# Attention scores by three one-pass matmuls of split q and k, with four float64 conversions moved behind the first two experts

## The chip, the cores and the metric

One core of a Trainium2 chip runs the whole program. The metric is the device time of one execution in microseconds; lower is better. TensorE is called PE here (its weight loads PEld), VectorE DVE, ScalarE ACT, GpSimd POOL, SyncE SP.

## The reference

Three layers run one after the other on 1792 tokens of 768 numbers. First an attention of 4 batches and 12 heads with a sigmoid in place of softmax, then a mixture of 8 experts to which tokens are given greedily by logit, 224 to each, then a dense layer with a squared relu:

```python
scores = scale * np.matmul(q, k.transpose(0, 1, 3, 2)) - np.log(S)   # q, k, v: (4, 12, 448, 64)
attn = 1.0 / (1.0 + np.exp(-scores))
x = np.matmul(attn, v)                      # then reshaped to (1792, 768)
...
h = np.maximum(x[mask] @ w1[e], 0.0)        # expert e, w1 (768, 1024), w2 (1024, 768)
out[mask] = h @ w2[e]
...
r = np.maximum(x @ w_in, 0.0)               # w_in (768, 2048), w_out (2048, 768)
out = (s * (r * r) + b) @ w_out
```

The weights of the dense layer, `w_in` and `w_out`, come as float64 bits; the kernel makes float32 of them itself, in 32 units of 128x768 numbers.

## The kernel before, in words

The program is written in one order (a manual schedule), and each engine runs its own instructions in that order. **Attention** is a loop over 24 head pairs i (6 pairs of each batch). A pair's q and k lie transposed with head 0 on partitions 0 to 63 and head 1 on 64 to 127, so a score matmul contracts over 64 rows, one half of the array for each head. In `scores` (L225) a chunk is 112 keys by 448 queries of both heads: two float32 matmuls on the two row halves (L235) into one PSUM tile `psc`, of which there are three, then one sigmoid on ACT (L236). A pair has four chunks. In `values` (L240) eight float32 matmuls make `pv` from the four chunks, and ACT copies it to `xT` (L253). Iteration i issues: the load of q and k of pair i+4, of v of pair i+3, `values(i)`, then the last two chunks of pair i+1 and the first two of pair i+2. The four chunks between two `values` are called a phase below.

In the same loop DVE makes float32 of the float64 units, `convert` (L155): four DVE instructions each (`to_float`, L148), a load of 768 KB ahead (`craw`) and a store of 384 KB behind (`nw`). The list CONV (L44) says how many in each iteration: 26 in all. The last LATE = 6 units are converted later (`late_convert`, L718), in one buffer called `orow`: its load is issued right behind the store of the conversion before.

After attention come the choice of experts, the gather of rows (`gather`, L531), and then four groups g. **A group** computes two experts, then the dense layer for their 448 tokens: 16 hidden blocks f (L743 to L761), each of 18 one-pass matmuls of 448 columns (L706 to L708), and two halves h of 8 spans (L768 to L797), each of 18 matmuls of 384 columns in group 0. All weights stream through SBUF in units: SP loads `raw` (L181), ACT rounds it to `wh` (L189, type float32r, one pass on PE), and `w_low` makes the rest `wl` = raw - wh (L200), on DVE for all units of the dense layer. `advance` (L666), called at the end of each block and span, keeps `wl` four units ahead of PE's use. Of a hidden block DVE also squares (L750) and makes the low part of `gt` (L755), which waits for ACT's high part (L754). In group 0 late conversions stand behind `advance` of blocks f = 1, 4, 7, 10, 13 and of the first span of half 0:

```python
advance()
if not g and f % 3 == 1:
    late_convert()
```

Unit 16 is that of the first span, unit 19 that of the fourth; block f's `advance` makes DVE split unit f + 4.

Of the kernel before, what the change touches and what calls it, by code (L numbers as in the profile page):

```python
# [8 lines left out]
F32 = mybir.dt.float32  # L9
F32R = mybir.dt.float32r  # L10
BF16 = mybir.dt.bfloat16
I32 = mybir.dt.int32
# [7 lines left out]
B, H, S, D = 4, 12, 448, 64  # L20
# [4 lines left out]
CP = 112  # L25
# [15 lines left out]
ROWS = (2, 2, 2, 2, 2, 2, 2, 2, 2, 2)  # L41
SYNC = 4
SIGNS = 2
CONV = [1, 1, 1, 1, 2] * 4 + [1, 1, 0]  # L44
LATE = 6
FULL = CAP - 0.5
BIG = 1.0e30
FLATC = 16384.0
# [14 lines left out]
def tile_kernel(ctx, tc, qT, kT, v, wg, w1, w2, wi, wo, s2, b2, cst, out):  # L63
    nc = tc.nc
    V, A, G, T = nc.vector, nc.scalar, nc.gpsimd, nc.tensor
# [51 lines left out]
    cgp = early.enter_context(tc.tile_pool(name="cgp", bufs=1))  # L117

    att = ExitStack()
    qk = att.enter_context(tc.tile_pool(name="qk", bufs=5))  # L120
    vp = att.enter_context(tc.tile_pool(name="vp", bufs=2))
    at = att.enter_context(tc.tile_pool(name="at", bufs=2))
    ps_s = att.enter_context(tc.tile_pool(name="ps_s", bufs=3, space=PSUM))
# [11 lines left out]
    def cv_in():  # L135
        if todo:
            i = todo.pop(0)
            src, k, n = wide[i]
            craw[i] = cgp.tile([128, 768, 2], I32, name="craw", bufs=3)
            nc.sync.dma_start(craw[i].rearrange("p a b -> p (a b)"), src[n].bitcast(I32).rearrange("p k c -> p (k c)"))  # L140
            coming.append(i)
# [64 lines left out]
        nu["use"] += 1  # L206
        return splits.pop(i)

    raw_qk, vt, attn, plg, lgs, pts = {}, {}, {}, {}, {}, {}
    pairs = [(b, p) for b in range(B) for p in range(NP)]  # L210

    def load_v(i):
        b, p = pairs[i]
        vt[i] = vp.tile([CP, NC, 128], F32, name="vt", bufs=5)
        nc.sync.dma_start(vt[i], v[b, p])

    def load_qk(i):
        b, p = pairs[i]
        rk = qk.tile([128, S], F32, name="rk")
        nc.sync.dma_start(rk, kT[b, p])  # L220
        rq = qk.tile([128, S], F32, name="rq")
        nc.sync.dma_start(rq, qT[b, p])
        raw_qk[i] = (rq, rk)

    def scores(n, c0, c1):  # L225
        if n >= len(pairs):
            return
        if c0 == 0:
            attn[n] = at.tile([CP, 2, NC, S], F32, name="attn")
        rq, rk = raw_qk[n]  # L230
        for c in range(c0, c1):
            p = ps_s.tile([CP, 2, 512], F32, name="psc")
            for j in range(2):
                me = slice(j * D, (j + 1) * D)
                T.matmul(p[:, j, :S], rk[me, c * CP:(c + 1) * CP], rq[me], start=True, stop=True)  # L235
            A.activation(attn[n][:, :, c, :], p[:, :, :S], AF.Sigmoid, bias=nls[:CP], scale=1.0 / math.sqrt(D))  # L236
        if c1 == NC:
            raw_qk.pop(n)

    def values(i):  # L240
        a, v = attn.pop(i), vt.pop(i)
# [95 lines left out]
    load_v(2)  # L337
    cv_in()
    cv_in()
    scores(0, 0, NC)  # L340
    scores(1, 0, 2)
    nc.sync.dma_start(sb2[:, 0:1], s2.partition_broadcast(128))
# [13 lines left out]
    for i in range(N):  # L356
        b, p = pairs[i]
        if i + 4 < N:
            load_qk(i + 4)
        if i + 3 < N:  # L360
            load_v(i + 3)
        values(i)
        scores(i + 1, 2, NC)
        scores(i + 2, 0, 2)
        if p == 0 and b:
            gate_turn(b - 1, True)
            prefs(b - 1)
        elif p == 4:
            gate(b, 0, 4 if b < B - 1 else 5, 6 if b < B - 1 else 5)
            if b == B - 1:  # L370
                gate_copy(b)
        elif p == 5 and b < B - 1:
            gate(b, 4, 6, 6)
            gate_copy(b)
        if b == B - 1 and 1 <= p <= 3:
            bracket(p - 1)
        if N - 6 <= i < N - 2:
            w_dma()
        if i >= N - 4:
            w_high()  # L380
            w_low(G)
        if i < N - 1:
            for _ in range(CONV[i]):
                convert()
# [343 lines left out]
        x_split(0, n)  # L728
    gather(1)
    row_ids()  # L730
    for g in range(4):
        y = ml.tile([128, KD, 2, S], F32R, name="y")
        expert(2 * g, y)
# [3 lines left out]
        if not t0:  # L737
            gt = ml.tile([128, KG, 2, 512], F32R, name="gt")
        gn = gt[:, :, :, t0:t0 + S]
        if not g:  # L740
            last["buf"] = ml.tile([128, 3072], I32, name="orow")
            late_in()
        for f in range(KG):  # L743
            wh, wl = w_get()
            p = ps_m.tile([128, 512], F32, name="acc")
            for k in range(KD):
                full_mm(p[:, :S], wh[:, k], wl[:, k], y, k, k == 0, k == KD - 1)
            r = m2p.tile([128, S], F32, name="r")
            A.activation(r, p[:, :S], AF.Relu)  # L749
            V.scalar_tensor_tensor(r, r, sb2[:, 0:1], r, op0=ALU.mult, op1=ALU.mult)  # L750
            if g:
                V.tensor_scalar(gn[:, f, 0], r, sb2[:, 1:2], None, op0=ALU.add)
            else:
                A.activation(gn[:, f, 0], r, AF.Identity, bias=sb2[:, 1:2])  # L754
            V.scalar_tensor_tensor(gn[:, f, 1], r, sb2[:, 1:2], gn[:, f, 0].bitcast(F32),  # L755
                                   op0=ALU.add, op1=ALU.subtract)
            if f % 4 == 3:
                x_split(2 * g + 2, f // 4)
            advance()
            if not g and f % 3 == 1:  # L760
                late_convert()  # L761
        gather(2 * g + 3)
        tiles = [(128 * t, idt[:, t - 1, g:g + 1]) for t in range(1, 4)]
# [4 lines left out]
        for h in range(2):  # L768
# [3 lines left out]
            for span in spans:  # L772
# [20 lines left out]
                        elif h:  # L793
                            out_rows.append((ids, orow[:, t]))
                advance()
                if not g and not h and span == [0]:
                    late_convert()  # L797


# [62 lines left out]
```

## Time and profile before

| what | value |
|---|---|
| time, median of 3 runs | 955.37 us (954.41 to 956.3) |
| the profiled execution's own time | 954.64 us |
| its span in the profile | 952.9 us |
| mean granted clock of PE | 0.976 |
| PE busy, share of the span | 926.7 us, 97% |
| weight loads (PEld) | 784.7 us, 82% |
| DVE | 554.8 us, 58% |
| ACT | 450.9 us, 47% |
| POOL | 137.7 us, 14% |

PE is busy nearly throughout, so the time is what PE has to run plus the stretches in which it waits. The shares of the other engines are means over stages: attention takes the first 170 us, the choice of experts some 45, the four groups the rest. Matmul records overlap (the next one starts before the last has left the array), so what one costs is read from the distance of starts, not from its duration.

### The profile page before, as it was taken

How to read it: one execution, taken by the hardware profiler on the slowest of the kernel's cores; microseconds unless marked ns; L12 is line 12 of the kernel's file. 1: busy time of each engine (PE TensorE's matmuls, PEld its weight loads, DVE VectorE, ACT ScalarE, POOL GpSimd, SP SyncE). 2: the span in 40 equal slices, each digit the busy share in tenths (PEclk: the TensorE clock that was granted, in tenths of full speed). 3: DMA queues.
4: the chain of work that ended last, by engine and by line, in shares of the span. 5: the costliest groups of instructions: out<-in, count | busy, mean ns of one | idle time of the engine just before them, and what ended most of it. 6: DMA issues, size and time to landing. Idle time of an engine off the chain costs nothing.

```text
span 952.9 us, 14071 instructions
## 1 busy us (share of the span) xinstructions
PE 926.7 (97%) x5277; PEld 784.7 (82%) x5277; DVE 554.8 (58%) x999; ACT 450.9 (47%) x787; POOL 137.7 (14%) x136
## 2 busy tenths in 40 slices
PE   9999999778999999999999999999999999999997
PEld 3333433557899999999999999999999999999997
DVE  3453736653876885387677223776773287777320
ACT  6665657644664443466433124664333366533120
POOL 1000001324410000433000003420000242100001
PEclk9999999758999999999999999999999999999999
DMA  9979776553675665477433324774444376443411
GB/s 294 376 251 367 277 278 237 151 157 134 206 225 183 218 213 192 143 240 230 146 116 117 125 87 138 244 230 131 119 127 145 119 240 207 136 132 103 128 36 66
DMA packets 68456, 173.08 MB, mean 182 GB/s; under 512 B 7968, under 2 KB 24864, under 8 KB 68384
## 3 DMA queue, kind: packets, MB, share of 16 engines
q1 hardware_dynamic: 64256, 160.22, 51.9%
q0 software_dynamic: 2272, 11.01, 3.4%
q10 hardware_dynamic: 1856, 0.92, 0.3%
q8 instruction: 42, 0.69, 0.3%
q14 instruction: 30, 0.25, 0.1%
HBM read 148.52 MB, written 23.59 MB: 181 GB/s over the span
## 4 chain that ended last, share of the span: by engine, by line
PE 84%; DVE 5%; DMA 5%; issue 2%; ACT 2%; POOL 1%; POOLq 0%; ACTq 0%; SPq 0%; DVEq 0%
PE acc L640 9%; PE acc L706 8%; PE acc L707 8%; PE acc L708 8%; PE psc L235 8%; PE acc L780 8%; PE acc L782 8%; PE acc L781 8%; PE pv L245 8%; PE acc L641 4%; DMA raw<-in_w_dram 4%; DVE wl L200 3%; PE px L407 2%; ACT wh L189 1%; DMA xr<-xs,idx 1%
## 5 line engine op out<-in xcount | busy, mean ns | idle before, releaser
L189 ACT CAST wh<-raw 128x768 fp32r<-128x768 f32 (+1 forms) x240 | 209.0, 878 | 155.8 <-PE acc L782 125.8
L200 DVE TENSOR_TENSOR wl<-raw,wh 128x768 fp32r<-128x768 f32 (+1 forms) x198 | 209.5, 1064 | 97.2 <-ACT wh L189 97.2
L200 POOL TENSOR_TENSOR wl<-raw,wh 128x768 fp32r<-128x768 f32 (+1 forms) x42 | 91.6, 2188 | 422.7 <-ACT wh L189 422.6
L780 PE MATMUL acc<-wh,gt 128*128 128x384 f32 x448 | 149.9, 335 | 0.0
L782 PE MATMUL acc<-wh,gt 128*128 128x384 f32 x448 | 149.7, 334 | 0.0
L781 PE MATMUL acc<-wl,gt 128*128 128x384 f32 x448 | 149.7, 334 | 0.0
L706 PE MATMUL acc<-y,wh 128*128 128x448 f32 x384 | 141.2, 368 | 0.0
L708 PE MATMUL acc<-y,wl 128*128 128x448 f32 x384 | 140.4, 366 | 0.0
L707 PE MATMUL acc<-y,wh 128*128 128x448 f32 x384 | 140.4, 366 | 0.0
L640 PE MATMUL acc<-u,wh 128*128 128x448 f32 x384 | 122.1, 376 | 3.5 <-DVE u L664 3.2
L641 PE MATMUL acc<-u,wl 128*128 128x224 f32 x384 | 101.5, 264 | 0.0
L236 ACT ACTIVATE attn<-psc,nls 112x896 f32<-112x896 f32 x96 | 89.0, 1009 | 13.7 <-PE psc L235 13.7
L640 PE MATMUL acc<-x,wh 128*128 128x448 f32 x288 | 95.2, 385 | 0.0
L749 ACT ACTIVATE r<-acc 128x448 f32<-128x448 f32 x64 | 34.8, 544 | 116.1 <-PE acc L708 116.1
L781 PEld LDWEIGHTS acc<-wl,gt 128*128 128x128 f32 x448 | 84.1, 188 | 0.0
L780 PEld LDWEIGHTS acc<-wh,gt 128*128 128x128 f32 x448 | 84.1, 188 | 0.0
L782 PEld LDWEIGHTS acc<-wh,gt 128*128 128x128 f32 x448 | 84.1, 188 | 0.0
L640 PEld LDWEIGHTS acc<-u,wh 128*128 128x128 f32 x384 | 72.0, 188 | 10.9 <-DVE u L664 5.7
L235 PE MATMUL psc<-rq,rk 64*112 64x448 f32 x384 | 78.8, 549 | 0.0
L641 PE MATMUL acc<-x,wl 128*128 128x224 f32 x288 | 77.2, 268 | 0.9 <-POOL wl L200 0.9
L245 PE MATMUL pv<-attn,vt 112*64 112x448 f32 x384 | 77.5, 545 | 0.0
L708 PEld LDWEIGHTS acc<-y,wl 128*128 128x128 f32 x384 | 72.1, 188 | 5.9
(207 smaller groups left out, 1223.2 us busy)
## 6 DMA issues: line engine op xcount, KB each, us to landing
raw<-nw SPq DMA_DIRECT2D x128, 384.0 KB, 3.1
raw<-in_w_dram SPq DMA_DIRECT2D x64, 384.0 KB, 3.2
raw<-in_w_dram SPq DMA_DIRECT2D x48, 512.0 KB, 4.4
craw<-in_wi_dram SPq DMA_DIRECT2D x16, 768.0 KB, 8.6
nw<-co SPq DMA_DIRECT2D x26, 384.0 KB, 7.5
craw<-in_wo_dram SPq DMA_DIRECT2D x10, 768.0 KB, 8.6
rk<-in_kT_dram SPq DMA_DIRECT2D x24, 224.0 KB, 8.4
rq<-in_qT_dram SPq DMA_DIRECT2D x24, 224.0 KB, 8.4
```

Of the source, the lines that this page charges most:

```text
L189: A.copy(h[:, :k], raws[i][:, :k])
L200: eng.tensor_sub(lo[:, :k], r[:, :k], h[:, :k].bitcast(F32))
L235: T.matmul(p[:, j, :S], rk[me, c * CP:(c + 1) * CP], rq[me], start=True, stop=True)
L245: T.matmul(pv[j * 64:(j + 1) * 64, :S], v[:, c, j * D:(j + 1) * D], a[:, j, c, :], start=(c == 0), stop=(c == NC - 1))
L640: T.matmul(p[:, :2 * CAP], wh[:, k], src[:, k].rearrange("p a s -> p (a s)"), start=(k == 0), stop=False)
L641: T.matmul(p[:, :CAP], wl[:, k], src[:, k, 0], start=False, stop=(k == n - 1))
L706: T.matmul(p, wh, src[:, k, 0], start=first, stop=False)
L707: T.matmul(p, wh, src[:, k, 1], start=False, stop=False)
L708: T.matmul(p, wl, src[:, k, 0], start=False, stop=last)
L780: T.matmul(ps[t][:, :DH], hi, wh[:, cols], start=(f == 0), stop=False)
L781: T.matmul(ps[t][:, :DH], hi, wl[:, cols], start=False, stop=False)
L782: T.matmul(ps[t][:, :DH], lo, wh[:, cols], start=False, stop=(f == KG - 1))
```

## The change

Of pairs 2 to 23, DVE splits q and k when they are loaded (`split_qk`): a high part in float32r and the low rest, both heads and both of q and k in one 128x896 instruction each, kept in the rings of the weight splits `wh` and `wl` (five tiles each). A chunk's two float32 matmuls become six in float32r: high by high, low k by high q, high k by low q, each on both row halves. Pairs 0 and 1 stay as they were. The split of pair i+3 stands at the start of iteration i, ahead of that iteration's conversion; q and k of a pair share one tile, four of them in the ring. CONV becomes one conversion in each of 22 iterations, LATE becomes 10: four more units are converted in group 0, behind blocks f = 0, 2, ..., 14 and behind spans 0 and 2 of the first half. The first late load is issued ahead of expert 0 and no longer behind expert 1.

```diff
@@ -41,8 +41,9 @@
 ROWS = (2, 2, 2, 2, 2, 2, 2, 2, 2, 2)
 SYNC = 4
 SIGNS = 2
-CONV = [1, 1, 1, 1, 2] * 4 + [1, 1, 0]
-LATE = 6
+CONV = [1] * 22 + [0]
+LATE = 10
+PLAIN = 2
 FULL = CAP - 0.5
 BIG = 1.0e30
 FLATC = 16384.0
@@ -117,7 +118,7 @@
     cgp = early.enter_context(tc.tile_pool(name="cgp", bufs=1))
 
     att = ExitStack()
-    qk = att.enter_context(tc.tile_pool(name="qk", bufs=5))
+    qk = att.enter_context(tc.tile_pool(name="qk", bufs=4))
     vp = att.enter_context(tc.tile_pool(name="vp", bufs=2))
     at = att.enter_context(tc.tile_pool(name="at", bufs=2))
     ps_s = att.enter_context(tc.tile_pool(name="ps_s", bufs=3, space=PSUM))
@@ -206,7 +207,7 @@
         nu["use"] += 1
         return splits.pop(i)
 
-    raw_qk, vt, attn, plg, lgs, pts = {}, {}, {}, {}, {}, {}
+    raw_qk, two_qk, vt, attn, plg, lgs, pts = {}, {}, {}, {}, {}, {}, {}
     pairs = [(b, p) for b in range(B) for p in range(NP)]
 
     def load_v(i):
@@ -216,26 +217,40 @@
 
     def load_qk(i):
         b, p = pairs[i]
-        rk = qk.tile([128, S], F32, name="rk")
-        nc.sync.dma_start(rk, kT[b, p])
-        rq = qk.tile([128, S], F32, name="rq")
-        nc.sync.dma_start(rq, qT[b, p])
-        raw_qk[i] = (rq, rk)
+        r = qk.tile([128, 2, S], F32, name="rqk")
+        nc.sync.dma_start(r[:, 1], kT[b, p])
+        nc.sync.dma_start(r[:, 0], qT[b, p])
+        raw_qk[i] = r
+
+    def split_qk(i):
+        r = raw_qk.pop(i)
+        h = wsp.tile([128, 8, 128], F32R, name="wh").rearrange("p k c -> p (k c)")[:, :2 * S]
+        lo = wlp.tile([128, 8, 128], F32R, name="wl").rearrange("p k c -> p (k c)")[:, :2 * S]
+        r = r.rearrange("p a s -> p (a s)")
+        V.tensor_copy(h, r)
+        V.tensor_sub(lo, r, h.bitcast(F32))
+        two_qk[i] = [a.rearrange("p (a s) -> p a s", a=2) for a in (h, lo)]
 
     def scores(n, c0, c1):
         if n >= len(pairs):
             return
         if c0 == 0:
             attn[n] = at.tile([CP, 2, NC, S], F32, name="attn")
-        rq, rk = raw_qk[n]
+        if n < PLAIN:
+            terms = [(raw_qk[n], raw_qk[n])]
+        else:
+            h, lo = two_qk[n]
+            terms = [(h, h), (lo, h), (h, lo)]
         for c in range(c0, c1):
             p = ps_s.tile([CP, 2, 512], F32, name="psc")
-            for j in range(2):
-                me = slice(j * D, (j + 1) * D)
-                T.matmul(p[:, j, :S], rk[me, c * CP:(c + 1) * CP], rq[me], start=True, stop=True)
+            for m, (kx, qx) in enumerate(terms):
+                for j in range(2):
+                    me = slice(j * D, (j + 1) * D)
+                    T.matmul(p[:, j, :S], kx[me, 1, c * CP:(c + 1) * CP], qx[me, 0], start=(m == 0),
+                             stop=(m == len(terms) - 1))
             A.activation(attn[n][:, :, c, :], p[:, :, :S], AF.Sigmoid, bias=nls[:CP], scale=1.0 / math.sqrt(D))
         if c1 == NC:
-            raw_qk.pop(n)
+            (raw_qk if n < PLAIN else two_qk).pop(n)
 
     def values(i):
         a, v = attn.pop(i), vt.pop(i)
@@ -337,6 +352,7 @@
     load_v(2)
     cv_in()
     cv_in()
+    split_qk(2)
     scores(0, 0, NC)
     scores(1, 0, 2)
     nc.sync.dma_start(sb2[:, 0:1], s2.partition_broadcast(128))
@@ -359,6 +375,8 @@
             load_qk(i + 4)
         if i + 3 < N:
             load_v(i + 3)
+        if i + 3 < N:
+            split_qk(i + 3)
         values(i)
         scores(i + 1, 2, NC)
         scores(i + 2, 0, 2)
@@ -728,6 +746,8 @@
         x_split(0, n)
     gather(1)
     row_ids()
+    last["buf"] = ml.tile([128, 3072], I32, name="orow")
+    late_in()
     for g in range(4):
         y = ml.tile([128, KD, 2, S], F32R, name="y")
         expert(2 * g, y)
@@ -737,9 +757,6 @@
         if not t0:
             gt = ml.tile([128, KG, 2, 512], F32R, name="gt")
         gn = gt[:, :, :, t0:t0 + S]
-        if not g:
-            last["buf"] = ml.tile([128, 3072], I32, name="orow")
-            late_in()
         for f in range(KG):
             wh, wl = w_get()
             p = ps_m.tile([128, 512], F32, name="acc")
@@ -757,7 +774,7 @@
             if f % 4 == 3:
                 x_split(2 * g + 2, f // 4)
             advance()
-            if not g and f % 3 == 1:
+            if not g and f % 2 == 0:
                 late_convert()
         gather(2 * g + 3)
         tiles = [(128 * t, idt[:, t - 1, g:g + 1]) for t in range(1, 4)]
@@ -793,7 +810,7 @@
                         elif h:
                             out_rows.append((ids, orow[:, t]))
                 advance()
-                if not g and not h and span == [0]:
+                if not g and not h and span in ([0], [2]):
                     late_convert()
```

How it moves instructions, at three places. First PE, one phase of attention ahead of a `values` (names: `psc` a score chunk, `rq`/`rk` q and k, `wh`/`wl` their high and low parts, `pv` the values). Before, two matmuls make a chunk:

```order
L245 MATMUL pv_345<-attn_280,vt_210 64x448 x8
L235 MATMUL psc_355<-rq_208,rk_206 112x448 x2
L235 MATMUL psc_359<-rq_208,rk_206 112x448 x2
L235 MATMUL psc_364<-rq_258,rk_256 112x448 x2
L235 MATMUL psc_368<-rq_258,rk_256 112x448 x2
```

and now six, in three steps of two row halves; here the first three of a phase's four chunks:

```order
L260 MATMUL pv_500<-attn_404,vt_311 64x448 x8
L249 MATMUL psc_510<-wh_374 112x448 x2
L249 MATMUL psc_510<-wh_374,wl_375 112x448 x2
L249 MATMUL psc_510<-wl_375,wh_374 112x448 x2
L249 MATMUL psc_518<-wh_374 112x448 x2
L249 MATMUL psc_518<-wh_374,wl_375 112x448 x2
L249 MATMUL psc_518<-wl_375,wh_374 112x448 x2
L249 MATMUL psc_527<-wh_435 112x448 x2
L249 MATMUL psc_527<-wh_435,wl_436 112x448 x2
L249 MATMUL psc_527<-wl_436,wh_435 112x448 x2
```

Nothing changes places on PE; each chunk has three pairs of matmuls for one.

Second DVE, iteration 12 of attention (`L` to `Wp` are the gate preferences of a batch, which wait for PE; `craw`, `co` a conversion's input and output). Before:

```order
L281 COPY L_88<-small_839 112x32
L285 TENSOR_TENSOR ge_845<-L_88 112x256
L287 TENSOR_REDUCE rank_846<-ge_845 112x32
L288 TENSOR_SCALAR Wp_89<-rank_846 112x32
L150 TENSOR_SCALAR co_850<-craw_711 128x768
L151 TENSOR_SCALAR cb__851<-craw_711 128x768
L152 SCALAR_TENSOR_TENSOR co_850<-craw_711,co_850 128x768
L153 ISA co_850<-co_850,cb__851 128x1536
```

and now (`rqk` is the raw q and k of pair 15):

```order
L230 CAST wh_1013<-rqk_943 128x896
L231 TENSOR_TENSOR wl_1014<-rqk_943,wh_1013 128x896
L296 COPY L_88<-small_1060 112x32
L300 TENSOR_TENSOR ge_1066<-L_88 112x256
L302 TENSOR_REDUCE rank_1067<-ge_1066 112x32
L303 TENSOR_SCALAR Wp_89<-rank_1067 112x32
L151 TENSOR_SCALAR co_1071<-craw_875 128x768
L152 TENSOR_SCALAR cb__1072<-craw_875 128x768
L153 SCALAR_TENSOR_TENSOR co_1071<-craw_875,co_1071 128x768
L154 ISA co_1071<-co_1071,cb__1072 128x1536
```

What moved: a split of two instructions stands ahead of the iteration's other work, the preferences and the conversion.

Third DVE in group 0, from the last hidden block (f = 15) into the spans of half 0 (`r`, `gt` the hidden values, `x` a later expert's rows, `wl` a unit's low part, `orow` a late conversion). Before:

```order
L750 SCALAR_TENSOR_TENSOR r_3683<-r_3683,sb2_76 128x448
L755 SCALAR_TENSOR_TENSOR gt_3156<-r_3683,sb2_76,gt_3156 128x448
L635 TENSOR_TENSOR x_3285<-px_3688,x_3285 128x3x96
L200 TENSOR_TENSOR wl_3696<-raw_3562,wh_3662 128x768
L200 TENSOR_TENSOR wl_3727<-raw_3592,wh_3698 128x768
L150 TENSOR_SCALAR orow_3157<-orow_3157 128x768
L151 TENSOR_SCALAR orow_3157<-orow_3157 128x768
L152 SCALAR_TENSOR_TENSOR orow_3157<-orow_3157 128x768
L153 ISA orow_3157<-orow_3157 128x1536
L200 TENSOR_TENSOR wl_3756<-raw_3622,wh_3729 128x768
L200 TENSOR_TENSOR wl_3780<-raw_3658,wh_3758 128x768
L200 TENSOR_TENSOR wl_3804<-raw_3694,wh_3782 128x768
```

and now, where the conversion behind span 2 begins in the last row:

```order
L767 SCALAR_TENSOR_TENSOR r_4081<-r_4081,sb2_76 128x448
L772 SCALAR_TENSOR_TENSOR gt_3538<-r_4081,sb2_76,gt_3538 128x448
L653 TENSOR_TENSOR x_3671<-px_4086,x_3671 128x3x96
L201 TENSOR_TENSOR wl_4094<-raw_3954,wh_4054 128x768
L201 TENSOR_TENSOR wl_4125<-raw_3984,wh_4096 128x768
L151 TENSOR_SCALAR orow_2752<-orow_2752 128x768
L152 TENSOR_SCALAR orow_2752<-orow_2752 128x768
L153 SCALAR_TENSOR_TENSOR orow_2752<-orow_2752 128x768
L154 ISA orow_2752<-orow_2752 128x1536
L201 TENSOR_TENSOR wl_4155<-raw_4020,wh_4127 128x768
L201 TENSOR_TENSOR wl_4179<-raw_4050,wh_4157 128x768
L151 TENSOR_SCALAR orow_2752<-orow_2752 128x768
```

The tenth conversion stands between the splits of units 22 and 23. Ahead of the first row shown there are eight late conversions now, and five before.

## Rows read from the trace of the kernel before

**Rows 1.** The chain that ended last, in order of time, attention: start us, us, what.

```profile
19.88 3.19 PE psc L235 x16
...
165.02 3.16 PE pv L245 x16
```

**Rows 2.** Windows, 20 to 160 us: busy us of each engine (instructions), clock, DMA.

```profile
20.00:160.00 140.00, 140.00 (x727) 53.81 (x727) 73.38 (x119) 91.20 (x110) 1.94 (x1) 1.00 0.87 310
```

**Rows 3.** L235, 19.8 to 24 us: its durations, then PE and PEld by time.

```profile
L235 PE MATMUL psc<-rq,rk x16: 536/536/627, 19.8 to 22.5; 64*112 64x448 f32 x16
...
19.81 0.63 PE L235 MATMUL psc<-rq,rk 64*112 64x448 f32 x2
...
20.28 0.18 PEld L235 LDWEIGHTS psc<-rq,rk 64*112 64x112 f32 x2 [0.20 <-issue]
...
21.41 0.18 PEld L235 LDWEIGHTS psc<-rq,rk 64*112 64x112 f32 x2 [0.20 <-issue]
21.93 0.41 PEld L235 LDWEIGHTS psc<-rq,rk 64*112 64x112 f32 x4 [0.34 <-ACT attn L236]
```

**Rows 4.** ACT by time in the same phase.

```profile
20.87 1.01 ACT L236 ACTIVATE attn<-psc,nls 112x896 f32<-112x896 f32 x1 [0.41 <-PE psc L235]
...
21.78 1.90 ACT L236 ACTIVATE attn<-psc,nls 112x896 f32<-112x896 f32 x2
```

**Rows 5.** PE by time, group 0's hidden blocks: a pass of 448 columns.

```profile
329.79 0.36 PE L708 MATMUL acc<-y,wl 128*128 128x448 f32 x1
...
331.61 0.36 PE L708 MATMUL acc<-y,wl 128*128 128x448 f32 x1
```

**Rows 6.** The page: low halves of weight units on DVE (mean ns).

```profile
L200 DVE TENSOR_TENSOR wl<-raw,wh 128x768 fp32r<-128x768 f32 (+1 forms) x198 | 209.5, 1064 | 97.2 <-ACT wh L189 97.2
```

**Rows 7.** DVE by time, one conversion of attention.

```profile
34.53 0.56 DVE L150 TENSOR_SCALAR co<-craw 128x768 int32<-128x768 int32 x1 [2.28 <-DMA nw<-co]
...
36.46 0.96 DVE L153 CUSTOM_DVE_ANT_0 co<-co,cb__462 128x1536 uint16<-128x1536 uint16 x1
```

**Rows 8.** PE by time: ends of group 0's hidden blocks and of its two halves.

```profile
287.36 0.38 PE L706 MATMUL acc<-y,wh 128*128 128x448 f32 x1
...
346.88 0.42 PE L780 MATMUL acc<-wh,gt 128*128 128x384 f32 x1
...
396.89 0.36 PE L640 MATMUL acc<-x,wh 128*128 128x448 f32 x1
```

**Rows 9.** DVE by time, group 0: hidden blocks, then the first half.

```profile
295.45 0.69 DVE L750 SCALAR_TENSOR_TENSOR r<-r,sb 128x448 f32<-128x448 f32 x1 [0.67 <-ACT r L749]
...
308.25 0.68 DVE L750 SCALAR_TENSOR_TENSOR r<-r,sb 128x448 f32<-128x448 f32 x1
...
313.94 0.68 DVE L750 SCALAR_TENSOR_TENSOR r<-r,sb 128x448 f32<-128x448 f32 x1
...
316.83 0.68 DVE L750 SCALAR_TENSOR_TENSOR r<-r,sb 128x448 f32<-128x448 f32 x1
...
354.10 0.45 DVE L635 TENSOR_TENSOR x<-px,x 128x288 fp32r<-128x288 f32 x1
354.47 1.82 DVE L200 TENSOR_TENSOR wl<-raw,wh 128x768 fp32r<-128x768 f32 x2
356.61 0.56 DVE L150 TENSOR_SCALAR orow<-orow 128x768 int32<-128x768 int32 x1 [0.32 <-DMA orow<-in_wo_dram]
```

**Rows 10.** SP by time, and DMA issues of 286 to 365 us (us to landing).

```profile
349.67 0.42 SPq L716 DMA_DIRECT2D orow<-in_wo_dram  x1
...
orow<-in_wo_dram SPq DMA_DIRECT2D x6, 768.0 KB, 4.8
```

**Rows 11.** PE by time, and windows with the clock, before expert 0.

```profile
217.81 0.42 PE L632 MATMUL acc<-ident,xr 96*128 96x96 f32 x1 [1.20 <-DMA xr<-xs,idx]
...
214.00:216.00 2.00, 0.00 (x0) 0.00 (x0) 0.00 (x0) 0.00 (x0) 0.17 (x1) 1.00 0.81 247
...
218.00:220.00 2.00, 2.00 (x10) 1.84 (x10) 0.71 (x2) 1.16 (x3) 0.53 (x1) 0.50 0.00 0
```


## The prediction

> **What bounds the kernel now.** I read the chain that ended last first, in order of time. In attention it is PE alone: a phase of score chunks takes 3.19 us, a `values` 3.16 us, one behind the other up to 168 us [rows 1]; the windows confirm it, PE being busy for all of 140 us while DVE is busy for 73 and ACT for 91 [rows 2]. In the groups PE is again without a gap: group 0's 16 hidden blocks start at 287.36 us, its 16 spans at 346.88, the next expert at 396.89 [rows 8]; that is 3.72 us a block and 3.13 us a span. So PE work saved in attention shortens the run, and whatever makes PE wait in group 0 lengthens it. The change does the first on purpose; what it does to the second is read from DVE's order there.
>
> **Scores, what is saved.** The two row halves work together: two matmuls of up to 627 ns lie within 0.63 us [rows 3], and three steps from one pair of weight loads to the next take 21.41 - 20.28 = 1.13 us, 0.376 each [rows 3]. A chunk has two such steps (a float32 matmul is two records), 0.75 us. The phase is then 0.09 us of exposed first load (627 against 536 ns) + 4 x 0.75 + 0.09 at the end = 3.19 [rows 1, 3].
>
> A chunk now has three steps of one float32r pass. Their price on half the array is in no row. The nearest row is the same pass of 448 columns on the whole array: nine steps in 331.61 - 329.79 = 1.82 us, 0.202 each [rows 5]. The other bound is half a float32 step, 0.188 [rows 3]. I take 0.202, as it is the same data type with a fresh load for each pass. A chunk is then 0.61 us and a phase would be 0.09 + 2.42 + 0.09 = 2.61. It can't quite be, because the fourth chunk needs the first one's PSUM tile back (there are three). Before, the first sigmoid started at 20.87, 1.06 after the phase's start [rows 3, 4], 0.22 behind its chunk's passes (0.09 + 0.75). Now it starts at 0.09 + 0.61 + 0.22 = 0.92, lasts 1.01 [rows 4], and the waiting load goes 0.05 later (21.88 to 21.93) [rows 3, 4]: 1.98. With 0.09 of load exposed the chunk streams from 2.07 and not from 1.91, and the phase ends at 2.07 + 0.61 + 0.09 = 2.77. Saved: 0.42 us. This is a new wait of 0.16 us on ACT; behind it on PE stands only that chunk and the next `values`, whose inputs are older. 21 full phases (iterations 1 to 21) give 8.8, two half phases 0.28 each (1.50 - 1.22): **9.4 us**. With 0.188 the same steps give 2.68 a phase, and 11.5 us in all.
>
> The Trainium skill speaks for the second: "TensorE: Matmul & The Clock Gate", section "Back-to-back issue gap", gives N/2.4 + 2.5 ns between starts, by which a pass of 448 columns is 189 ns and the saving 11.4 us; this case's row shows 202 for such a pass, so I keep 202.
>
> **Splits, what is added on DVE.** 22 casts and 22 subtractions of 128x896. A subtraction scaled from the mean of those on weights, mostly 768 wide, is 1.06 x 7/6 = 1.24 us [rows 6]; a cast lies between 0.65 (0.56 x 7/6, a one-input operation) [rows 7] and 1.24. With a conversion of 2.89 us (34.53 to 37.42) [rows 7] an iteration asks 4.8 to 5.4 us of DVE, and PE takes 2.77 + 3.16 = 5.93. So the splits are hidden behind PE; without that cover they cost 22 x 1.9 = 42 us at least. A split is used one iteration later, which leaves some 10 us of slack. SP's order of q, k and v is kept; q and k are now wanted an iteration sooner, but four conversions less are 4.6 MB less where DMA was 0.87 busy [rows 2]. Cost: nothing; gain of the removed conversions: nothing either, DVE had waited there (2.28 us in one row) [rows 7].
>
> **Group 0, what is added.** In steady state DVE needs 2.89 us for a block (313.94 to 316.83, with the wait for ACT in it) and 2.80 for a late conversion (308.25 to 313.94, less 2.89) [rows 9]. With one behind every second block that is 4.29 a block against PE's 3.72; DVE falls behind all the way. The question is whether the lead of four units covers it. Before, the split of unit 19 ended near 354.47 + 0.91 = 355.38 [rows 9], and the fourth span wanted it at 346.88 + 3 x 3.13 = 356.26 [rows 8]: a slack of 0.9 us and no more. Now three more conversions stand ahead of it: 8.40, less the 0.67 for which DVE idled at the second block [rows 9], which the first conversion now fills, less 0.9: unit 19 is 6.8 us late, and PE has waited that long by then, in pieces (late blocks, second and fourth span).
>
> Then the ninth and tenth conversion. A late load lands 4.8 us after issue [rows 10], 5.3 after the end of the conversion before, whose store is issued first (I take its issue as long as the load's, 0.42 [rows 10]). Between the eighth and the ninth DVE has a block (2.89), a row split (0.37) and a unit (0.9), 4.2 in all [rows 9], so it waits 1.1. From the split of unit 19 to that of unit 23 it needs 0.9 + 1.1 + 2.8 + 5.3 + 2.8 + 0.9 = 13.8; PE runs four spans in 12.5. Another 1.3 us: **8.1 us** in all. The waiting conversion holds up every split queued behind it on DVE, and through them PE. Bounds: with loads that never make DVE wait 6.8; with each load as slow as the slowest shown (issued 349.67, still awaited until 356.61, 6.9 us) [rows 9, 10] a pair of blocks costs DVE 6.9 + 0.5 + 2.8 = 10.2 in place of 8.6, some 9 us more over seven pairs: 17.
>
> **The first late load, moved.** It now starts while expert 0's rows are gathered; the queues are 0.81 busy there, and PE waits for the rows for 1.20 us [rows 11]. The cost lies between nothing (it lands before or after) and half of its 4.8 us, 2.4; I take **0.3**, since only the gather's tail should meet it.
>
> **Sum.** -9.4 + 8.1 + 0.3 = -1.0 us on the profiled execution's 954.64: 953.6. The median of the runs is 0.73 above that execution, so I expect **954.4 us** against 955.37. A difference of 0.2% (1.9 us) is about what can be told from none here, so this is no change: two large terms that nearly cancel.
>
> **Rivals.**
> - *The passes run at 0.188* and the late loads are quick. For it: two float32 steps on halves cost exactly their columns. Against: rows 5. Terms -11.5, 6.8 and 0.3: 951.0. Chance 0.20.
> - *Group 0 absorbs the conversions.* Then only 9.4 is left, 946.3. Against: the 0.9 us of slack, 8.4 us of new work on a queue that never idles in between. Chance 0.07.
> - *Slow late loads.* Contention with the weight loads makes each take 6.9. It decides from 5.8 us behind the last conversion's end, which is what two blocks give (2 x 2.89); the median of 5.3 leaves 0.5. Group 0 then costs 17: 963.3, slower. Against: the median of the six is 4.8 [rows 10]. Chance 0.12.
> - *PE's clock falls in the new waits.* After waits of which the last was 1.20 us, the clock stood at 0.50 from 218 us [rows 11]; group 0 will have waits of 2 to 3 us. One or two spans at the lower level (1.2 GHz of 2.4) cost 3 to 6 us, half of it hidden by the later wait for DVE: about 957.5. Against: PE works 3 us or more between the waits. Chance 0.12.
> - *The passes don't overlap their loads, or the halves don't run together.* If each step shows 0.09 of load, the phase is 12 x 0.293 + 0.09 = 3.6, longer than 3.19: 9.6 lost for 9.4 saved, 973.4. Against: loads for both halves start with the matmuls and cost nothing before [rows 3]. Chance 0.04.
>
> Beside the last one stands a rule of the Trainium skill: the same page, section "Part 3: Packing small matmuls — row/col tiling", says that a weight load overlaps running matmuls only where its row group differs. By that the time would be this rival's; but the float32 steps would show their loads as well, and the rows show none.
>
> **How the numbers follow.** The forecast has the remaining 0.45, with a range of its own from 952.5 to 956.5, as the pass may be a little under 0.202 and the moved load dear or free. Faster than 953.5: 0.20 + 0.07 + 0.09 of the forecast = 0.36. Slower than 957.3: 0.12 + 0.04 + 0.07 of the clock's share = 0.23. The rest, 0.41, is no change. The range of 949.5 to 959 leaves out the absorbed case, the exposed loads and most of the slow late loads, 0.2 together.
>
> **What would show it.** In the changed profile a phase of 2.7 to 2.8 us with a wait for ACT ahead of its fourth chunk, attention ending near 159 us, DVE splits of 1.9 to 2.5 us with PE never waiting for them; in group 0 PE waits for `wl` from DVE of some 7 to 8 us, the largest at the fourth span. A phase of 2.68 says the first rival. No PE wait in group 0, or one over 12 us, would make the middle of the forecast wrong; so would a score phase over 3 us.

## The result, and the profile after

The changed kernel takes **961.21 us** (median of five runs, 958.62 to 962.57), the kernel before 954.41 in five runs beside it (952.09 to 956.30): a ratio of **1.0056** with a 95% interval of 1.0037 to 1.0076. (The two medians lie 0.71% apart; the ratio fits the 955.37 of the table ahead of the prediction better than the 954.41, and I go by the ratio.) It is slower, by more than can be taken for noise, and lies 2.2 us above the top of the range; the forecast was 954.4. The execution profiled after is the one of 961.21 us, with a span of 959.4 and a mean granted clock of 0.968, where it was 952.9 and 0.976.

I compare the two traces by the first matmul of each stage. Of the changed kernel, PE by time: the choice of experts, expert 0, group 0's hidden blocks, and expert 2.

```profile
159.55 0.41 PE L425 MATMUL px<-ident,xT 128*112 128x128 f32 x2
...
209.71 0.74 PE L658 MATMUL acc<-x,wh 128*128 128x448 f32 x1
...
277.60 0.38 PE L724 MATMUL acc<-y,wh 128*128 128x448 f32 x1
...
401.19 0.36 PE L658 MATMUL acc<-x,wh 128*128 128x448 f32 x1
```

Of the kernel before, the first two of these; the other two are in [rows 8].

```profile
169.70 0.30 PE L407 MATMUL px<-ident,xT 128*112 128x128 f32 x1
...
219.54 0.74 PE L640 MATMUL acc<-x,wh 128*128 128x448 f32 x1
```

Attention ends 10.15 us earlier, and 9.76 of that are still there when group 0's hidden blocks begin. From there to expert 2 the kernel before takes 396.89 - 287.36 = 109.53 us, the changed one 401.19 - 277.60 = 123.59: **14.06 us lost**. Attention was sized rightly; group 0 gave the lead back and 4.3 us more. The two profiled executions lie 6.6 us apart (961.21 and 954.64), so 2.3 us are lost behind group 0: 3.3 in the experts of group 2, where a stretch of 3.41 us at a granted clock of 0.50 stands from 642.6 us on, and some regained later. No other run shows that stretch, so I put no cause to it.

**Attention after.** The chain of waits shows the phase at 2.77 us where it was 3.19 [rows 1], the weight loads by time show its steps, and the windows show who is busy.

```profile
24.88 2.77 PE psc L249 x24
```

```profile
25.11 0.17 PEld L249 LDWEIGHTS psc<-wl,wh 64*112 64x112 f32 x2
...
26.35 0.17 PEld L249 LDWEIGHTS psc<-wl,wh 64*112 64x112 f32 x2
26.79 0.17 PEld L249 LDWEIGHTS psc<-wh 64*112 64x112 f32 x2 [0.27 <-ACT attn L251]
```

```profile
20.00:160.00 140.00, 140.00 (x953) 70.76 (x950) 100.46 (x152) 95.92 (x117) 6.97 (x4) 1.00 0.82 279
```

Six steps in 26.35 - 25.11 = 1.24 us are 0.207 each, and ahead of the fourth chunk stands the wait for ACT: 26.79 - 26.35 is 0.23 more than a step, where 0.16 was foreseen. The last row says that PE was busy for all of the 140 us, so it never stood idle for the splits, which cost DVE 626 and 1093 ns a pair:

```profile
L231 DVE TENSOR_TENSOR wl<-rqk,wh 128x896 fp32r<-128x896 f32 x20 | 21.9, 1093 | 0.7
...
L230 DVE CAST wh<-rqk 128x896 fp32r<-128x896 f32 x20 | 12.5, 626 | 17.4 <-DMA rqk<-in_qT_dram 16.5 <-PE small L275 0.8
```

**Group 0 after.** The waits of PE from 277 to 402 us (us in total, times, the longest), then windows: the hidden blocks, the halves, and two short stretches inside them. In the kernel before PE worked through both parts.

```profile
PE acc L726 <- DVE wl L201: 5.0, 4, 2.0
PE acc L798 <- DVE wl L201: 3.9, 2, 2.4
```

```profile
277.60:344.90 67.30, 62.34 (x302) 56.08 (x301) 48.44 (x71) 27.02 (x46) 1.38 (x1) 0.97 0.58 194
344.90:401.20 56.30, 52.40 (x292) 51.49 (x291) 30.79 (x41) 18.45 (x26) 5.08 (x3) 0.97 0.64 209
325.16:328.57 3.41, 3.41 (x11) 3.00 (x11) 3.38 (x6) 1.11 (x2) 0.00 (x0) 0.50 0.52 173
359.29:362.70 3.41, 3.41 (x13) 3.41 (x12) 2.28 (x4) 0.76 (x2) 0.00 (x0) 0.50 0.86 308
```

Two things stand there. PE waits 8.9 us for `wl`. That is near the 8.1 of the forecast, but by chance, as a wait costs more than its figure. This one shows it, PE by time:

```profile
303.69 0.37 PE L725 MATMUL acc<-y,wh 128*128 128x448 f32 x1
305.75 0.47 PE L726 MATMUL acc<-y,wl 128*128 128x448 f32 x1 [1.70 <-DVE wl L201]
306.06 0.36 PE L724 MATMUL acc<-y,wh 128*128 128x448 f32 x1
...
325.56 0.58 PE L724 MATMUL acc<-y,wh 128*128 128x448 f32 x1
...
328.18 0.55 PE L725 MATMUL acc<-y,wh 128*128 128x448 f32 x1
```

The starts lie 2.06 and 0.31 apart where 0.205 is usual: 1.96 lost for a wait called 1.70. Six waits of 8.9 us so cost some 10.5. And the mean clock of both windows is 0.97: behind the waits ending at 323.86 and 358.89 stands a stretch of 3.41 us each at a granted clock of 0.50 (1.2 GHz of 2.4). From 325.56 to 328.18 seven passes take 0.374 each; over 3.41 us that keeps back 3.41 x (1 - 0.205/0.374) = 1.5 us of PE's work, some 3.0 for the two.

That is where PE's time went; it doesn't say yet what set the time. PE needs the low part of unit 23 at span 7, the last span of half 0. DVE splits that unit right behind the tenth conversion, and PE's weight load still waits for it there (DVE's splits of units 23 on, then PEld):

```profile
372.16 3.56 DVE L201 TENSOR_TENSOR wl<-raw,wh 128x768 fp32r<-128x768 f32 x4
```

```profile
373.17 0.19 PEld L798 LDWEIGHTS acc<-wl,gt 128*128 128x128 f32 x1 [0.27 <-DVE wl L201]
```

From the start of that split to the end of the stage are 401.19 - 372.16 = 29.03 us. In the kernel with the conversions alone, below, they are 410.79 - 381.75 = 29.04, with one stretch of half clock in place of two. So DVE set the time: what the clock took from PE ahead of span 7 only shortened the wait that PE would have had there, and the two stretches cost the stage next to nothing.

**The second conversion.** DVE by time, then SP by time, of the changed kernel:

```profile
286.86 0.96 DVE L154 CUSTOM_DVE_ANT_0 orow<-orow 128x1536 uint16<-128x1536 uint16 x1
...
289.75 1.82 DVE L201 TENSOR_TENSOR wl<-raw,wh 128x768 fp32r<-128x768 f32 x2
...
299.46 0.56 DVE L151 TENSOR_SCALAR orow<-orow 128x768 int32<-128x768 int32 x1 [5.00 <-DMA orow<-in_wo_dram]
```

```profile
290.77 0.32 SPq L182 DMA_DIRECT2D raw<-nw  x1
291.14 1.11 SPq L740 DMA_DIRECT2D nw<-orow  x1
292.30 0.43 SPq L734 DMA_DIRECT2D orow<-in_wo_dram  x1
```

The first conversion ends at 286.86 + 0.96 = 287.8. Its store could go then, and the next load behind it; both go only from 291.14 on. Ahead of them on SP is a load of weights (290.77), issued by the same block's `advance`, that waits for a `raw` buffer. DVE splits only one unit in block 0 and then two in block 1 (289.75); SP goes on when the first of these two is split and its buffer free. So the second late load is issued 4.5 us behind the end of the first conversion (in the kernel with the first conversion ahead, below, it is 0.4) and lands late, and DVE stands still for 5.0 us with every split queued behind it.

The Trainium skill says of the path from GpSimd that such a wait happens on the issuing sequencer, ahead of dispatch ("DMA: Bandwidth & Descriptors", section "Anatomy of one DMA — SWDGE (gpsimd) path"). This trace agrees for SP, with 3.3 us between the end of the conversion and the issue of its store.

### The profile page after: what moved, and what is told of

The parts are those of the page before. It is cut to its first block, busy times and chain, and to the rows that moved or that the text cites. A ratio compares the mean times of both kernels' runs of the same rounds, so it can differ in the third digit from the quotient of the medians.

```text
span 959.4 us, 14490 instructions
## 1 busy us (share of the span) xinstructions
PE 923.4 (96%) x5453; PEld 802.9 (84%) x5453; DVE 590.5 (62%) x1043; ACT 449.4 (47%) x787; POOL 138.3 (14%) x136
## 4 chain that ended last, share of the span: by engine, by line
PE 81%; DVE 8%; DMA 4%; issue 2%; ACT 2%; POOL 1%; SPq 0%; POOLq 0%; ACTq 0%; DVEq 0%
PE acc L658 12%; PE pv L260 8%; PE acc L798 8%; PE acc L799 8%; PE acc L797 8%; PE psc L249 7%; PE acc L724 6%; PE acc L726 6%; PE acc L725 6%; PE acc L659 6%; DVE wl L201 3%; DMA raw<-in_w_dram 2%; PE px L425 2%; DMA orow<-in_wo_dram 1%; ACT gt L771 1%
## 5 line engine op out<-in xcount | busy, mean ns | idle before, releaser
L725 PEld LDWEIGHTS acc<-y,wh 128*128 128x128 f32 x384 | 72.7, 189 | 5.8
```

Of the source, the lines that this page charges most:

```text
L725: T.matmul(p, wh, src[:, k, 1], start=False, stop=False)
```

## The experiments

My theory was that the change is two terms that add, attention's gain and group 0's loss, and that the loss has three parts: DVE's own work, late loads (the held second one first), and PE's clock. The rivals were that the terms depend on each other, that the held load is made up for later, and that the clock costs nothing as DVE sets the time.

**The scores alone.** The change with the conversions of before:

```diff
-CONV = [1] * 22 + [0]
-LATE = 10
+CONV = [1, 1, 1, 1, 2] * 4 + [1, 1, 0]
+LATE = 6
...
-            if not g and f % 2 == 0:
+            if not g and f % 3 == 1:
                 late_convert()
...
-                if not g and not h and span in ([0], [2]):
+                if not g and not h and span == [0]:
```

(with the first late load back where it was.)

> The scores and splits of the change, with the conversions placed as before (26 in attention, 6 late). Theory (attention and group 0 are two terms that add): attention ends 9.8 us earlier, group 0 takes 109.5 us as before, and the whole is 954.4 - 9.8 = 944.6 us (943 to 947). Rival (taking four conversions out of attention is what made room for the splits on DVE, in SBUF or in the queues): with 26 conversions DVE is asked for 4.8 us an iteration on average and 7.6 where two stand in one, against 5.93 of PE; PE then waits in some of the four iterations with two, up to 1.7 us each, and the whole is 948 to 952.

Measured: 945.27 us, ratio to before **0.9909** (0.9894 to 0.9925). Its window of attention, then its group 0 by time:

```profile
20.00:160.00 140.00, 140.00 (x954) 70.99 (x951) 112.36 (x167) 96.22 (x117) 6.44 (x4) 1.00 0.92 313
```

```profile
277.50 0.38 PE L724 MATMUL acc<-y,wh 128*128 128x448 f32 x1
...
387.03 0.36 PE L658 MATMUL acc<-x,wh 128*128 128x448 f32 x1
```

Group 0 takes 109.53 us, to the hundredth what it took before, and PE waits for nothing there. In attention DVE is busy for 112 of 140 us and the queues at 0.92, and PE still works all the time. So the splits needed no room made for them. This is the fastest kernel of all that ran.

**The conversions alone.** The kernel before with CONV, LATE, the places and the first late load of the change.

> Scores as before; only the ten late conversions of the change, with the first late load moved as there. Theory (group 0's loss is the conversions' own): group 0 loses the 14 us that it lost in the changed kernel, 954.4 + 14 = 968.4 us (966.5 to 970.5), with waits of PE for wl near 9 us and two stretches of half clock. The prediction's own price, 8.1 + 0.3, would give 962.8. Rival (part of the 14 us comes from the new scores: group 0 starts with other queues and another clock): about 963 to 966.

Measured: 967.25 us, ratio 1.0136 (1.0119 to 1.0153). Its group 0, by time, then its waits in the spans and the split of unit 23 on DVE:

```profile
288.06 0.38 PE L706 MATMUL acc<-y,wh 128*128 128x448 f32 x1
...
410.79 0.36 PE L640 MATMUL acc<-x,wh 128*128 128x448 f32 x1
```

```profile
PE acc L780 <- DVE wl L200: 5.9, 3, 2.4
```

```profile
381.75 3.56 DVE L200 TENSOR_TENSOR wl<-raw,wh 128x768 fp32r<-128x768 f32 x4
```

122.73 us, 13.2 more than before, with one stretch of half clock where two were expected. The terms add within the noise: -0.91% and +1.36% against +0.56% together. The loss belongs to the moved conversions.

**The late transfers on POOL.** `late_in` and the late store issue by `G.dma_start` and not by `nc.sync.dma_start`.

> The changed kernel with the ten late loads and stores issued by POOL and not by SP. Theory (the second conversion waited 5.0 us because its load stood on SP behind a load of weights that waited for a buffer): that wait falls to 1 us or less, DVE is some 4 us less late at the first waits, PE's waits for wl fall from 8.9 to about 5, and the whole to 957 us (955.5 to 958.5). Rival (the second conversion's wait only took up idle time that DVE would have had anyway): no change, 960.5 to 962. A third case: POOL issues so slowly that later loads come late, and the time rises above 962.

Measured: 965.85 us, ratio 1.0128 (1.0112 to 1.0143): the third case. DVE's conversions, by time (second and tenth), and POOL's ninth store and tenth load:

```profile
296.30 0.56 DVE L151 TENSOR_SCALAR orow<-orow 128x768 int32<-128x768 int32 x1 [1.18 <-DMA orow<-in_wo_dram]
...
372.31 0.56 DVE L151 TENSOR_SCALAR orow<-orow 128x768 int32<-128x768 int32 x1 [7.46 <-DMA orow<-in_wo_dram]
```

```profile
357.03 1.70 POOL L555 DMA_INDIRECT xr<-xs,idx  x1 [0.30 <-issue]
...
363.97 0.59 POOL L734 DMA_DIRECT2D orow<-in_wo_dram  x1
```

The second wait fell from 5.0 to 1.18, as the theory had it. But the tenth load, behind the gather of rows on the same queue, took 372.31 - 363.97 = 8.3 us, PE waited 12.7 us in the stage (3.7 in the blocks, 9.0 in the spans), and group 0 took 405.83 - 278.29 = 127.54. What slowed that load isn't shown. The run is no test of the hold by the time, so the next one removes the hold without another queue.

**PE's waits filled.** 32 small matmuls on zeros where PE waited:

```diff
+    def fill(n):
+        if n:
+            p = ps_x.tile([128, 3, 128], F32, name="px").rearrange("p a b -> p (a b)")
+            for _ in range(n):
+                T.matmul(p, zs[:, :128], zs[:, :384], start=True, stop=True)
...
+            if not g:
+                fill({7: 6, 9: 2, 11: 8, 15: 2}.get(f, 0))
...
+                if not g and not h:
+                    fill({1: 5, 3: 9}.get(span[0], 0))
```

> The changed kernel with small matmuls on zeros put on PE in front of hidden blocks 7, 9, 11, 15 and spans 1 and 3 of the first half in group 0, 32 in all of some 0.16 us, where PE waited for wl; their results are not used. Theory (the two stretches of half clock in group 0 are a term of their own, 1.7 us each): the clock stays at 1.00 from 277 to 400 us, the waits of PE without these matmuls stay as long as they were or grow by 1.7 in the spans, and the whole is 1.7 to 3.4 us shorter, 957.8 to 959.5. Rival (the clock falls cost nothing, as DVE sets the time): 960.5 to 962. If the clock still falls, the stretch has another cause than the idle time ahead of it.

Measured: 958.86 us, ratio 1.0054 (1.0035 to 1.0073), which can't be told from the changed kernel's 1.0056. That is no gain that the time shows. The window of its group 0, the second conversion and the split of unit 23 on DVE, and the first of the small matmuls on PE:

```profile
278.30:399.40 121.10, 116.34 (x623) 107.44 (x622) 79.28 (x111) 45.60 (x72) 6.03 (x4) 1.00 0.61 205
```

```profile
297.82 0.56 DVE L152 TENSOR_SCALAR orow<-orow 128x768 int32<-128x768 int32 x1 [2.66 <-DMA orow<-in_wo_dram]
...
370.35 3.56 DVE L202 TENSOR_TENSOR wl<-raw,wh 128x768 fp32r<-128x768 f32 x4
```

```profile
304.20 1.15 PE L750 MATMUL px<-zs 128*128 128x384 bf16 x6
```

The clock stays at 1.00, and the stage takes 399.39 - 278.33 = 121.06 us, 2.5 less than in the changed kernel. But this is not the clock's: the second late load landed sooner in this execution. DVE waited 2.66 us for it, and the second conversion begins 19.5 us behind the start of the stage, where it is 21.9 in the changed kernel (299.46 - 277.60). This lead of 2.4 us stands there 6 us before the first small matmul runs, and DVE keeps it to the split of unit 23, from whose start to the end of the stage it is again 29.04 us. So the rival holds, that the falls cost nothing as DVE sets the time. That 958.86 lies in the range of the theory is no support for the theory, as by the ratios, each against the kernel before run beside it, there is no gain. With PE's idle time filled the clock doesn't fall. That idle time is the cause is likely by this run and the second one with fills, below; here the waits were also shorter by the earlier load.

**The first conversion ahead.**

```diff
+            if not g and f == 0:
+                late_convert()
             advance()
-            if not g and f % 2 == 0:
+            if not g and f and f % 2 == 0:
                 late_convert()
```

> The changed kernel with the first late conversion, its store and the second late load put ahead of that block's load of weights instead of behind it. Theory (that load waits on SP for a buffer until 291 us and holds the store and the second late load 3.4 us, which makes DVE wait 5.0): the second conversion waits under 1.5 us, the waits of PE at blocks 7 and 9 go, that at block 11 shrinks, those at the spans stay; group 0 loses 8 to 10.5 us where it lost 14.1, the whole takes 955 to 958 us. Rival (group 0's loss is DVE's work and the later loads; the early hold is made up for): 960.5 to 962, and group 0 loses 13 us or more.

Measured: 955.00 us, ratio **0.9993** (0.9976 to 1.0011). SP and DVE by time:

```profile
287.36 0.42 SPq L734 DMA_DIRECT2D orow<-in_wo_dram  x1
287.90 6.96 SPq L182 DMA_DIRECT2D raw<-nw  x4
```

```profile
294.39 0.55 DVE L151 TENSOR_SCALAR orow<-orow 128x768 int32<-128x768 int32 x1
...
348.72 0.56 DVE L151 TENSOR_SCALAR orow<-orow 128x768 int32<-128x768 int32 x1 [1.49 <-DMA orow<-in_wo_dram]
...
365.84 0.56 DVE L151 TENSOR_SCALAR orow<-orow 128x768 int32<-128x768 int32 x1 [4.42 <-DMA orow<-in_wo_dram]
...
368.65 3.56 DVE L201 TENSOR_TENSOR wl<-raw,wh 128x768 fp32r<-128x768 f32 x4
```

One statement moved past `advance` for one block, and the second conversion waits for nothing; the load that was ahead of it on SP now waits behind it, and PE waits for no unit before block 13. Group 0 takes 120.47 us, **10.9** above before and 3.1 below the changed kernel. PE waits for `wl` 7.1 us (1.7 in the blocks, 5.4 in the spans), and not at blocks 7, 9 and 11. The loss is 0.4 above the 8 to 10.5 expected, and the clock can account for it: from the last microsecond of the longest wait on, 4.0 us at span 3, the clock is at 0.50 for the whole of this window, and from the start of unit 23's split to the end of the stage it is 398.09 - 368.65 = 29.44 us where it is 29.04 elsewhere:

```profile
354.00:360.80 6.80, 5.88 (x18) 5.88 (x19) 5.70 (x8) 2.22 (x3) 0.00 (x0) 0.50 0.67 234
```

**One load only.**

```diff
         last["i"] += 1
-        late_in()
```

> The changed kernel with one late load only: all ten late conversions work on the first unit's data and are stored as before, so that the weights of nine late units are wrong. DVE's work stays, all its waits for late loads go. Theory (DVE's own work sets 6.8 us, as the prediction had it as the lower bound): waits of PE for wl of 6.5 to 7.5 us, all at blocks 13 and 15 and spans 1 and 3; with one stretch of half clock at most, group 0 loses 7 to 9 us, the whole takes 954 to 956.5 us. Rival (the loads' waits are the most of it): group 0 loses under 4 us, the whole takes 951 or less.

Measured: 952.68 us, ratio 0.9963 (0.9949 to 0.9977). Its waits in group 0:

```profile
PE acc L797 <- DVE wl L201: 3.9, 2, 2.4
PE acc L726 <- DVE wl L201: 1.7, 2, 1.4
```

Four waits of 5.6 us, at blocks 13 and 15 and spans 1 and 3, as expected, and somewhat less than the 6.5 expected in that view; with what each wait costs on top the stage takes 116.79 us, 7.3 above before. No stretch of half clock falls into it. The whole is 1.3 us below the 954 to 956.5 expected, and above the rival's 951; in its trace the stages behind group 0 take 1.6 us less than before, which is no part of this question.

**The fills with the first conversion ahead**, 5 small matmuls at block 15, 5 at span 1 and 16 at span 3, otherwise as above.

> The kernel with the first late conversion put ahead, and 26 small matmuls on zeros in PE's remaining waits: 5 ahead of hidden block 15, 5 ahead of span 1 and 16 ahead of span 3 of the first half (some 0.16 us each; the longest wait there was 4.0 us). Theory (the 6.8 us of half clock behind that wait cost 2.6 us and hid about half of the wait for the tenth conversion): the clock stays at 1.00, a wait of 1 to 1.5 us appears at span 7, group 0 loses 9.3 to 10 us where it lost 10.9, and the whole is about 1.3 us shorter. Rival 1 (the fall is a cost in full): group 0 loses 8.3. Rival 2 (the later wait takes it all): 10.9.

Measured: 954.44 us, ratio 1.0002 (0.9989 to 1.0015); by the time alone no difference from the kernel without them. By the window, clock 1.00 and 118.3 us; then PE at span 7, and DVE's split of unit 23:

```profile
277.30:395.60 118.30, 115.17 (x616) 107.10 (x615) 79.11 (x111) 45.59 (x72) 6.34 (x4) 1.00 0.63 210
```

```profile
367.61 0.44 PE L812 MATMUL acc<-wl,gt 128*128 128x384 f32 x1 [0.81 <-DVE wl L202]
```

```profile
366.61 3.55 DVE L202 TENSOR_TENSOR wl<-raw,wh 128x768 fp32r<-128x768 f32 x4
```

The stage is 120.47 - 118.36 = 2.1 us shorter and loses 8.8, between the theory's 9.3 to 10 and the 8.3 of the full price. Most of that is again not the clock's: DVE waited 1.7 us less for the late loads (5.3 for the eighth to the tenth, where it was 7.0 without the fills), and unit 23's split begins 89.32 us behind the start of the stage (366.61 - 277.29) where it was 91.03. What is left for the clock is 0.4 us, and PE waits at span 7 instead (0.81 us, a start 1.14 us behind the one before). Whether the fills have to do with the earlier landing of those loads isn't shown.

**Two raw buffers**, with the first conversion ahead:

```diff
         last["i"] += 1
-        late_in()
+        late_in(i + 2)
...
-    late_in()
+    last["raw"] = [last["buf"][:, :1536], ml.tile([128, 1536], I32, name="lraw")]
+    late_in(last["i"])
+    late_in(last["i"] + 1)
```

> The kernel with the first late conversion put ahead, and a second buffer for the raw late units, so that each late load is issued two conversions ahead. Nothing is left out. Theory (the chain of conversion, store and load through one buffer costs 3.7 us, the difference between the two kernels before): DVE waits under 1.5 us in all for late loads, group 0 loses 7 to 8.5 us, the whole takes 952 to 954 us, between the forecast and the kernel with the scores alone. Rival (with two loads ahead the loads of weights behind them on SP come late, and PE waits for those): group 0 loses 10 us or more.

Measured: 953.43 us, ratio 0.9985 (0.9963 to 1.0007), with the whole computation. DVE waits for no late load any more (0.7 us for a store are left), and the clock stays up:

```profile
277.70:393.90 116.20, 110.77 (x591) 104.83 (x590) 78.84 (x111) 45.80 (x72) 6.33 (x4) 1.00 0.62 207
```

116.19 us (393.87 - 277.68) are **6.7** above before. That is what ten conversions in place of six cost by DVE's work alone.

## Why the prediction was wrong, step by step

By the traces' group 0 (109.53 us before), the experiments split the 14.06 us. The clock's share is read from the end of the stage against the start of unit 23's split, and the 0.4 us of it in the kernel with the first conversion ahead are left out of the two rows that use that kernel:

| what | kernels | us | forecast |
|---|---|---|---|
| DVE's own work | two raw buffers, over before | 6.7 | 6.8 |
| late loads through one buffer | first ahead, over two raw buffers | 3.9 | 1.3 |
| the held second late load | changed, over first ahead | 3.5 | none |
| PE's clock behind the waits | changed; first ahead | 0; 0.4 | rival, 0.12 |

Each row rests on one execution of each kernel, and the landing of a late load differs between them: for the held second one DVE waited 5.0, 3.5 and 2.7 us in three kernels with the same hold. So the second and third row are good to about 1 us.

- **Bound and scores: right.** PE was the bound of attention; the phase is 2.77 us, as worked out, with the wait for ACT ahead of the fourth chunk. 9.4 us were forecast; attention ends 9.5 to 10.2 earlier in the traces with the new scores. That the phase comes out to the hundredth is in part luck: the price of a pass, 0.202, was 0.005 too low, twelve times a phase, the wait for ACT 0.07 too low, and the 0.18 at the phase's two ends too high by about as much. The rival of 0.188 fell, and so did that of exposed loads: the steps show none.
- **Splits: right in that they are hidden**, and a little cheaper than forecast, 1.72 us a pair and not 1.9 to 2.5. That taking four conversions out of attention gains nothing was right too, and the scores alone show it.
- **DVE's own work in group 0: right**, 6.8 against 6.7, with the unit of the fourth span as the one that comes too late (5.4 us of the 6.7 stand as waits in that trace, the rest is what each wait costs on top).
- **The held load: the step that failed.** I wrote that a late load lands "5.3 after the end of the conversion before, whose store is issued first". This took SP to be free. The change moved the first conversion from block 1 to block 0, and there SP has a load of weights ahead of the store that waits for a buffer of DVE's. Of the first blocks the forecast said only that the first conversion fills 0.67 us of idle time; in fact the second late load had landed only 11.6 us after that end (299.46 - 287.82), and DVE waited 5.0 us for it. Putting the conversion ahead of that load gives back 3.1 us in group 0, and takes the ratio from 1.0056 to 0.9993. That this is 954.7 us against the 955.37, and so the forecast's 954.4 almost exactly, is in part luck, as group 0 still loses 10.9 there where 8.1 was forecast.
- **The clock: a rival that came true in the clock and not in the time.** "PE works 3 us or more between the waits" was the argument against it, and it isn't enough: the clock fell twice. I gave it 0.12, and half of 3 to 6 us as its cost, the other half being hidden by the later wait for DVE. In the changed kernel all of it was hidden, and in the kernel with the first conversion ahead all but 0.4 us.
- **The moved first late load: nothing, where 0.3 was taken.** Expert 0 starts 0.32 us later against the choice of experts than before; with the new scores and the old place of the load it is 0.36, so the move costs nothing that shows.
- **The late loads behind that: undersized.** 1.3 us were forecast for the ninth and tenth conversion; with the first conversion ahead the late loads cost 3.9, as the eighth conversion waits too (1.49 us there) and the tenth load lands 5.8 us behind its issue (360.09 to 365.84) where 4.8 was taken.
- **The rival of slow late loads was added up wrongly.** Seven pairs at 10.2 in place of 8.6 us are 11.2 and not 9 more, so its bound of 17 should have been 18, and its time 964.3 and not 963.3. The loads were slower than forecast, but not as slow as there.

With the measured terms the sum is -9.8 + 14.1 = +4.3 at expert 2, which is what the trace of the changed kernel shows there. The whole came out at +0.56%, 5.3 us (3.5 to 7.3 by the interval); the 1 us between them is below what these runs can tell.

## What to carry to other kernels

When a change moves a step that stores and loads, list what stands ahead of it on the issuing queue at the new place, and whether that entry itself waits for a buffer; one blocked load delays every transfer behind it. When an engine waits for another one, look for the last place where it waits: time that it loses ahead of that place, here by its clock, costs nothing, as the wait is shorter by as much, as long as the other engine doesn't wait for it in turn. When one execution of a stage is shorter than another, look whether the lead stands there before the edit acts. Of two halves of a change, run each alone: here one was worth 0.9%, and the other gave back more than that.

## What the runs showed of the hardware that I had not expected

- PE's granted clock fell to 0.50 behind waits of 1.97 and 2.42 us in the changed kernel, with other waits close ahead, for 3.41 us each; with one of 4.0 us it stood there for 6.8 us, from the last microsecond of the wait on. With one load only, with two raw buffers and with the conversions alone, a wait of 2.4 us at the same span had no such stretch behind it. What decides between them isn't shown.
- A wait of PE costs some 0.26 us more than its figure here (1.96 for one of 1.70), and such a cost, like that of a fall of the clock, vanishes when a later wait for the same engine follows.
- A float32r pass of 448 columns on half the array is 0.207 us from start to start, a little more than the 0.202 on the whole array [rows 5], with a weight load of 0.17 to 0.18 us beside it that costs nothing. The Trainium skill's N/2.4 + 2.5 ns ("TensorE: Matmul & The Clock Gate", section "Back-to-back issue gap", which calls it the gap of isolated matmuls) gives 189 ns. The traces don't agree, and the measurement decides; with the prediction's steps the page's figure would make the phase some 0.09 us shorter than it is.
